# Warm-up matmuls moved behind a data-dependent branch, and GpSimd's row-number copies moved into the first expert's second half

## The chip, the cores and the metric

The kernel runs on one core of a Trainium2 chip. The metric is the device time of one execution in microseconds (us). Three runs of the kernel before gave 944.73, 944.86 and 948.75; the median is 944.86. The engines are named as the profile names them: PE is TensorE (PEld its weight loads), DVE is VectorE, ACT is ScalarE, POOL is GpSimd, SP is SyncE, which here only issues DMAs.

## What is computed

Attention with a sigmoid feeds a layer of eight experts, in which each token goes to exactly one expert by a greedy global ranking, and that feeds a two-matrix block. All inputs and outputs are float32. The parts that matter:

```python
scores = scale * np.matmul(q, k.transpose(0, 1, 3, 2)) - np.log(S)
attn = 1.0 / (1.0 + np.exp(-scores))
x = np.matmul(attn, v)                  # laid out as 1792 tokens x 768
logits = x @ w_gate                     # 8 experts
for idx in np.argsort(-logits.flatten()):
    tok, e = idx // E, idx % E
    if assigned[tok] >= 0 or counts[e] >= cap:   # cap = 224
        continue
    assigned[tok] = e; counts[e] += 1
for e in range(E):
    h = np.maximum(x[assigned == e] @ w1[e], 0.0)
    out[assigned == e] = h @ w2[e]
r = np.maximum(out @ w_in, 0.0)
y = (s * (r * r) + b) @ w_out
```

## The kernel before

The kernel is one long program, placed by hand: every engine works through its instructions in the order in which the source issues them, and semaphores join the engines. Three stages follow each other.

**Attention** (lines 331 to 407, 0 to 165 us). 24 pairs of heads go through scores on PE, a sigmoid on ACT, and values on PE. The first thing that PE does is `keep_clock(WARM[0], ...)`, seven matmuls of zeros whose result nobody reads; the first scores stand behind them.

**Routing** (lines 409 to 620, 165 to 205 us). An auction of ten steps finds the assignment, `places` turns it into row numbers `idx`, and `gather(0)` lets POOL issue two indirect DMAs that fetch the 224 rows of expert 0 into `xr`. Then stands a branch, `go_on`: each engine loads `flag` from memory, and where the auction has not ended (it has, in this profile) the code behind the branch goes on with it. On the way past, each engine adds to its own semaphore what the skipped code would have added (the event semaphores of line 607), so that counts agree on both ways; an instruction behind the branch that waits for DVE's count therefore waits until DVE is past the branch too. Between `places` and the branch PE has `keep_clock(WARM[1], ...)`, 18 matmuls of zeros (line 563).

**Experts and the block** (from line 747, 205 us to the end). Four groups; each has two experts and then the two-matrix block for their 448 rows. Weights are units that come in one fixed order: 8 units of `w1` and 6 of `w2` for an expert, then 32 units of the block. A unit is loaded from memory into `raw` (four buffers), rounded on ACT to `wh` (line 190), and the remainder `wl = raw - wh` is taken on DVE or POOL (line 201), by the table `where`: POOL takes numbers 0, 2, 4, 6 and 12 of an expert's 14 units. A `raw` buffer is free for the next load when its `wl` is done. `advance` issues these steps, always with the unit that is four or five ahead of PE; the units 0 to 3 are split earlier, in the attention, and POOL takes their `wl` there whatever the table says.

In an expert, step f of the first half multiplies unit f with the expert's transposed rows `x` (lines 661, 662; the last two steps lines 680 to 682) and step d of the second half multiplies unit 8 + d with `u`. `x_split(e, n)` transposes a piece of `xr` on PE and splits it on ACT and DVE (lines 653 to 656); expert 0's four pieces stand ahead of its first step, and expert 1's pieces n = 0 to 3 stand behind steps f = 1 to 4 of expert 0, in two buffers `px` of PSUM. Ahead of expert 0 stand `gather(1)` and `row_ids()`. `row_ids` (line 629) is 16 small copies on POOL of `idx` into `idt` and `idl`, which the scatters of finished rows read; the first scatter comes with expert 2.

Of the kernel before, what the change touches and what calls it, by code (L numbers as in the profile page):

```python
# [8 lines left out]
F32 = mybir.dt.float32  # L9
F32R = mybir.dt.float32r  # L10
BF16 = mybir.dt.bfloat16
# [13 lines left out]
CP = 112  # L25
NC = S // CP
NCH = NT // CP
NP = H // 2
KD = DM // 128
KF = F1 // 128  # L30
# [6 lines left out]
STEPS = 10  # L37
MORE = (3, 8)
AHEAD = (2, 3, 4, 5)
WARM = (7, 18, 4, 4)  # L40
ROWS = (3, 3, 2, 2, 2, 2, 2, 2, 2, 2)
SYNC = 0
SIGNS = 2
# [20 lines left out]
def tile_kernel(ctx, tc, qT, kT, v, wg, w1, w2, wi, wo, s2, b2, cst, out):  # L64
# [3 lines left out]
    const = ctx.enter_context(tc.tile_pool(name="const", bufs=1))  # L68
# [17 lines left out]
    ep = early.enter_context(tc.tile_pool(name="ep", bufs=1))  # L86
# [79 lines left out]
    units, where = [], []  # L166
    for g in range(4):
        for e in (2 * g, 2 * g + 1):
            units += [(w1[e, f], KD, True) for f in range(KF)]
            units += [(w2[e, d], KF, True) for d in range(KD)]  # L170
            where += [n in (0, 2, 4, 6, 12) for n in range(KF + KD)]
        units += [(narrow[i], wide[i][1], False) for i in range(len(wide))]
        where += [False] * len(wide)
    raws, splits = {}, {}
# [153 lines left out]
            V.tensor_copy(dv[0][:, 1:], mm[:, 0:1].to_broadcast([128, LEVELS]))  # L328
            V.tensor_scalar(th, kvec, dv[0][:, 1:2], dv[0][:, 0:1], op0=ALU.mult, op1=ALU.add)

    zero = ep.tile([128, 512], BF16, name="zero")
    V.memset(zero, 0.0)

    def keep_clock(n, p):
        for _ in range(n):
            T.matmul(p, zero[:, :CP], zero, start=True, stop=True)

    keep_clock(WARM[0], ps_s.tile([CP, 2, 512], F32, name="psc")[:, 0])
    warm = ep.tile([1, 1], F32, name="warm")
# [32 lines left out]
    for i in range(N):  # L372
        b, p = pairs[i]
# [38 lines left out]
    ps_t = rt.enter_context(tc.tile_pool(name="ps_t", bufs=3, space=PSUM))  # L412
# [147 lines left out]

    auction(STEPS, True)
    places(lambda: rows(len(turns)))
    keep_clock(WARM[1], ps_t.tile([CP, NC, 128], F32, name="px").rearrange("p c n -> p (c n)"))
    def greedy():
        mk = rp.tile([128, CP], F32, name="mk")
        cand = rp.tile([128, CP], F32, name="cand")
# [58 lines left out]
    ps_m = ctx.enter_context(tc.tile_pool(name="ps_m", bufs=6, space=PSUM))  # L625
# [3 lines left out]
    def row_ids():  # L629
        def put(dst, rows, h, col, r0, n, src):  # L630
            for r in range(0, n, 32):
                G.tensor_copy(dst[rows + r:rows + r + 32, col], idx[r0 + r:r0 + r + 32, h, src])

        a, b = slice(0, E, 2), slice(1, E, 2)
        put(idt[:, 0], 0, 0, slice(0, 4), 64, 64, a)
        put(idt[:, 0], 64, 1, slice(0, 4), 0, 64, a)
        put(idt[:, 1], 0, 1, slice(0, 4), 64, 32, a)
        put(idt[:, 1], 32, 0, slice(0, 4), 0, 96, b)
        put(idt[:, 2], 0, 0, slice(0, 4), 96, 32, b)
        put(idt[:, 2], 32, 1, slice(0, 4), 0, 96, b)  # L640
        put(idl, 0, 0, slice(0, 2), 0, 64, slice(0, E, 4))
        put(idl, 64, 0, slice(0, 2), 0, 64, slice(2, E, 4))
# [15 lines left out]
    def half_mm(wh, wl, src, n, func, dst, ahead):  # L658
        p = ps_m.tile([128, 512], F32, name="acc")
        for k in range(n):  # L660
            T.matmul(p[:, :2 * CAP], wh[:, k], src[:, k].rearrange("p a s -> p (a s)"), start=(k == 0), stop=False)  # L661
            T.matmul(p[:, :CAP], wl[:, k], src[:, k, 0], start=False, stop=(k == n - 1))  # L662
        bs = m2p.tile([128, CAP], F32, name="bs")
        A.copy(bs, p[:, CAP:2 * CAP])
        tt = m2p.tile([128, CAP], F32, name="tt")
        V.tensor_add(tt, p[:, :CAP], bs)
        if ahead:
            advance()
        hi, lo = dst
        if func == AF.Relu:  # L670
            A.activation(hi, tt, func)
            V.scalar_tensor_tensor(lo, tt, 0.0, hi.bitcast(F32), op0=ALU.max, op1=ALU.subtract)
        else:
            A.copy(hi, tt)
            V.tensor_sub(lo, tt, hi.bitcast(F32))  # L675
# [19 lines left out]
    def expert(e, y):  # L695
        x = xg.pop(e)
        u = ml.tile([128, KF, 2, CAP], F32R, name="u")
        for f in range(KF):
            wh, wl = w_get()
            if f < KF - 2:  # L700
                half_mm(wh, wl, x, KD, AF.Relu, (u[:, f, 0], u[:, f, 1]), f < KF - 3)
                if f == KF - 3:
                    advance()
            else:
                short_mm(wh, wl, x, KD, (u[:, f, 0], u[:, f, 1]))
                if f == KF - 2:
                    advance()
            if 1 <= f <= 4:
                if e % 2 == 0:
                    x_split(e + 1, f - 1)  # L710
                if out_rows:
                    scatter(*out_rows.pop(0))
        sl = slice((e % 2) * CAP, (e % 2 + 1) * CAP)
        for d in range(KD):
            wh, wl = w_get()
            half_mm(wh, wl, u, KF, AF.Copy, (y[:, d, 0, sl], y[:, d, 1, sl]), d < KD - 1)

    def scatter(ids, row):
        G.memset(spacer, 0.0)
# [25 lines left out]
        late_in()  # L745

    stores, out_rows = [], []
    for n in (0, 2, 1, 3):
        x_split(0, n)
    gather(1)  # L750
    row_ids()
    last["buf"] = ml.tile([128, 3072], I32, name="orow")
    late_in()
    for g in range(4):
# [8 lines left out]
        for f in range(KG):  # L763
            wh, wl = w_get()
            p = ps_m.tile([128, 512], F32, name="acc")
# [22 lines left out]
        for h in range(2):  # L788
            ps = [ps_m.tile([128, 512], F32, name="acc") for _ in tiles]
            n = KG // 2  # L790
# [91 lines left out]
```

## Time and profile before

| what | value |
|---|---|
| median of three runs | 944.86 us |
| the profiled execution, device time | 946.52 us |
| its span, first to last instruction | 944.7 us |
| mean granted clock of PE | 0.983 |
| PE matmuls busy | 917.0 us (97%) |
| PE weight loads busy | 797.0 us (84%) |
| DVE / ACT / POOL busy | 587.6 / 449.3 / 138.1 us |

All times in the rows below are from the profiled execution, which took 946.52 us: 944.7 us of span and 1.8 us around it. Its granted clock is a share of full speed: 1.00 is 2.4 GHz and 0.50 is 1.2 GHz. The page's busy time for PE holds matmuls that wait in its pipeline and so says little about how near PE is to its peak; a stage is read by what its engines wait for.

### The profile page before, as it was taken

To read this page: it belongs to the slowest core of one execution; us is meant where nothing else is said; L and a number is where in the kernel's file an instruction comes from. 1 tells how busy PE (TensorE), PEld (TensorE's weight loads), DVE (VectorE), ACT (ScalarE), POOL (GpSimd) and SP (SyncE) were. 2 spreads that over 40 slices of the span, in tenths; PEclk is the share of its full clock that TensorE was granted. 3 is DMA by queue.
4 is the path that set the end of the run, shared out by engine and by line. 5 is a ranking of instruction groups with operands and counts; after the bars stand their busy time and mean duration, and the time that the engine had idled before them with its cause. 6 is when DMAs were issued, how large, how long until landed. Compare 5 with 4: busy or idle time off the path is not lost.

```text
span 944.7 us, 14521 instructions
## 1 busy us (share of the span) xinstructions
PE 917.0 (97%) x5467; PEld 797.0 (84%) x5467; DVE 587.6 (62%) x1043; ACT 449.3 (48%) x787; POOL 138.1 (15%) x136
## 2 busy tenths in 40 slices
PE   9999999688999999999999999999999999999997
PEld 4454555568999999999999999999999999999997
DVE  3877875645868875578776224786773287777320
ACT  6666767735654432566333225564332366433120
POOL 1000003224410000442000004420000232100001
PEclk9999999779999999999999999999999999999999
DMA  9989993844746666567334235763444476433311
GB/s 307 321 298 341 321 323 111 241 134 167 239 144 214 219 230 217 179 222 230 119 117 141 90 101 165 232 218 122 129 127 137 119 251 211 137 120 108 126 34 68
DMA packets 68459, 173.12 MB, mean 183 GB/s; under 512 B 7968, under 2 KB 24864, under 8 KB 68384
## 3 DMA queue, kind: packets, MB, share of 16 engines
q1 hardware_dynamic: 66112, 161.13, 52.9%
q0 software_dynamic: 2272, 11.01, 3.4%
q8 instruction: 44, 0.72, 0.3%
q14 instruction: 31, 0.25, 0.1%
HBM read 148.52 MB, written 23.59 MB: 182 GB/s over the span
## 4 chain that ended last, share of the span: by engine, by line
PE 56%; DVE 10%; DMA 5%; ACT 3%; issue 2%; POOL 1%; POOLq 0%; SPq 0%; ACTq 0%; DVEq 0%
PE acc L661 9%; PE acc L801 7%; PE acc L802 7%; PE acc L800 7%; PE acc L727 6%; PE acc L728 6%; PE acc L729 6%; PE acc L662 4%; DVE wl L201 4%; DMA raw<-in_w_dram 3%; DMA orow<-in_wo_dram 2%; ACT wh L190 1%; DVE y L675 1%; ACT gt L774 1%; DVE r L770 1%
## 5 line engine op out<-in xcount | busy, mean ns | idle before, releaser
L190 ACT CAST wh<-raw 128x768 fp32r<-128x768 f32 (+1 forms) x240 | 208.8, 877 | 160.6 <-PE acc L802 115.7
L201 DVE TENSOR_TENSOR wl<-raw,wh 128x768 fp32r<-128x768 f32 (+1 forms) x198 | 207.2, 1053 | 91.1 <-ACT wh L190 91.1
L201 POOL TENSOR_TENSOR wl<-raw,wh 128x768 fp32r<-128x768 f32 (+1 forms) x42 | 92.6, 2213 | 414.8 <-ACT wh L190 414.7
L801 PE MATMUL acc<-wl,gt 128*128 128x384 f32 x448 | 150.4, 336 | 1.8 <-DVE wl L201 1.8
L800 PE MATMUL acc<-wh,gt 128*128 128x384 f32 x448 | 150.6, 336 | 0.0
L802 PE MATMUL acc<-wh,gt 128*128 128x384 f32 x448 | 150.4, 336 | 0.0
L727 PE MATMUL acc<-y,wh 128*128 128x448 f32 x384 | 141.4, 368 | 0.0
L729 PE MATMUL acc<-y,wl 128*128 128x448 f32 x384 | 140.6, 366 | 0.0
L728 PE MATMUL acc<-y,wh 128*128 128x448 f32 x384 | 140.6, 366 | 0.0
L661 PE MATMUL acc<-u,wh 128*128 128x448 f32 x384 | 121.9, 376 | 1.8 <-DVE u L685 1.5
L662 PE MATMUL acc<-u,wl 128*128 128x224 f32 x384 | 101.4, 264 | 0.0
L661 PE MATMUL acc<-x,wh 128*128 128x448 f32 x288 | 94.4, 383 | 0.7 <-DVE x L656 0.7
L251 ACT ACTIVATE attn<-psc,nls 112x896 f32<-112x896 f32 x96 | 88.8, 1008 | 9.4 <-PE psc L249 9.4
L769 ACT ACTIVATE r<-acc 128x448 f32<-128x448 f32 x64 | 34.8, 543 | 116.7 <-PE acc L729 116.7
L801 PEld LDWEIGHTS acc<-wl,gt 128*128 128x128 f32 x448 | 84.7, 189 | 2.1 <-DVE wl L201 2.1
L800 PEld LDWEIGHTS acc<-wh,gt 128*128 128x128 f32 x448 | 84.7, 189 | 0.0
L802 PEld LDWEIGHTS acc<-wh,gt 128*128 128x128 f32 x448 | 84.5, 189 | 0.0
L662 PE MATMUL acc<-x,wl 128*128 128x224 f32 x288 | 76.8, 267 | 3.0 <-POOL wl L201 3.0
L661 PEld LDWEIGHTS acc<-u,wh 128*128 128x128 f32 x384 | 72.1, 188 | 8.9 <-DVE u L685 3.6
L260 PE MATMUL pv<-attn,vt 112*64 112x448 f32 x384 | 77.5, 545 | 0.0
L729 PEld LDWEIGHTS acc<-y,wl 128*128 128x128 f32 x384 | 72.1, 188 | 6.3
L728 PEld LDWEIGHTS acc<-y,wh 128*128 128x128 f32 x384 | 72.2, 188 | 6.1
(212 smaller groups left out, 1306.7 us busy)
## 6 DMA issues: line engine op xcount, KB each, us to landing
raw<-nw SPq DMA_DIRECT2D x128, 384.0 KB, 3.0
raw<-in_w_dram SPq DMA_DIRECT2D x64, 384.0 KB, 3.9
raw<-in_w_dram SPq DMA_DIRECT2D x48, 512.0 KB, 4.5
craw<-in_wi_dram SPq DMA_DIRECT2D x16, 768.0 KB, 5.8
nw<-co SPq DMA_DIRECT2D x24, 384.0 KB, 7.7
craw<-in_wo_dram SPq DMA_DIRECT2D x8, 768.0 KB, 6.3
orow<-in_wo_dram SPq DMA_DIRECT2D x8, 768.0 KB
rqk<-in_kT_dram SPq DMA_DIRECT2D x24, 224.0 KB, 6.9
```

The source lines that it names most:

```text
L190: A.copy(h[:, :k], raws[i][:, :k])
L201: eng.tensor_sub(lo[:, :k], r[:, :k], h[:, :k].bitcast(F32))
L251: A.activation(attn[n][:, :, c, :], p[:, :, :S], AF.Sigmoid, bias=nls[:CP], scale=1.0 / math.sqrt(D))
L260: T.matmul(pv[j * 64:(j + 1) * 64, :S], v[:, c, j * D:(j + 1) * D], a[:, j, c, :], start=(c == 0), stop=(c == NC - 1))
L661: T.matmul(p[:, :2 * CAP], wh[:, k], src[:, k].rearrange("p a s -> p (a s)"), start=(k == 0), stop=False)
L662: T.matmul(p[:, :CAP], wl[:, k], src[:, k, 0], start=False, stop=(k == n - 1))
L727: T.matmul(p, wh, src[:, k, 0], start=first, stop=False)
L728: T.matmul(p, wh, src[:, k, 1], start=False, stop=False)
L729: T.matmul(p, wl, src[:, k, 0], start=False, stop=last)
L800: T.matmul(ps[t][:, :DH], hi, wh[:, cols], start=(f == 0), stop=False)
L801: T.matmul(ps[t][:, :DH], hi, wl[:, cols], start=False, stop=False)
L802: T.matmul(ps[t][:, :DH], lo, wh[:, cols], start=False, stop=(f == KG - 1))
```

## The change

Four edits, none of which changes what is computed.

1. `WARM[0]` goes from 7 to 5.
2. The zero matmuls of `WARM[1]` move from ahead of the branch to behind it, directly ahead of expert 0's transposes, and go from 18 to 14. Their operand `zero` moves to a pool that lives that long, and their result goes to a buffer of the experts' PSUM pool.
3. `row_ids()` moves from ahead of expert 0 to behind step d = 1 of expert 0's second half.
4. In the table `where`, POOL gives expert 0's units 0, 2 and 4 to DVE and keeps 6 and 12. Since units 0 to 3 are split in the attention with POOL named outright, unit 4 alone changes its engine.

```diff
-WARM = (7, 18, 4, 4)
+WARM = (5, 14, 4, 4)
...
-            where += [n in (0, 2, 4, 6, 12) for n in range(KF + KD)]
+            where += [n in ((0, 2, 4, 6, 12) if e else (6, 12)) for n in range(KF + KD)]
...
-    zero = ep.tile([128, 512], BF16, name="zero")
+    zero = const.tile([128, 512], BF16, name="zero")
...
     auction(STEPS, True)
     places(lambda: rows(len(turns)))
-    keep_clock(WARM[1], ps_t.tile([CP, NC, 128], F32, name="px").rearrange("p c n -> p (c n)"))
...
             half_mm(wh, wl, u, KF, AF.Copy, (y[:, d, 0, sl], y[:, d, 1, sl]), d < KD - 1)
+            if not e and d == 1:
+                row_ids()
...
+    keep_clock(WARM[1], ps_m.tile([128, 512], F32, name="acc")[:CP])
     for n in (0, 2, 1, 3):
         x_split(0, n)
     gather(1)
-    row_ids()
```

On PE, where the routing ends. Before: the last matmul of `places`, the first zero matmul, the load of the flag and the branch; the skipped code; and the first transpose of expert 0 behind it (the semaphores in brackets are named by engine or DMA queue).

```order
L544 MATMUL pi_2242<-R_1803,oh_1804 96x16
L336 LDWEIGHTS zero_170
L336 MATMUL px_2279<-zero_170 112x512
...
L606 TENSOR_LOAD flag_1798 [waits DMAHW4_49,DMAHW3_49,DMAHW5_49,DMAHW2_49,DMAHW6_49,DMAHW1_49,DMAHW7_49,DMAHW0_49,DVE_49]
L607 COMPARE_AND_BRANCH
...
L653 MATMUL acc_2742<-ident_75,xr_2298 128x128 [waits DMASW0_49,DVE_49,DMASW2_49,PE_49,Activation_49]
```

After, at the same place:

```order
L544 MATMUL pi_2240<-R_1801,oh_1802 96x16
L605 TENSOR_LOAD flag_1796 [waits DMAHW4_49,DMAHW3_49,DMAHW5_49,DMAHW2_49,DMAHW6_49,DMAHW1_49,DMAHW7_49,DMAHW0_49,DVE_49]
L606 COMPARE_AND_BRANCH
...
L336 LDWEIGHTS zero_170 [waits DVE_49,PE_49]
L336 MATMUL acc_2720<-zero_170 112x512 [waits Activation_49]
...
L652 MATMUL acc_2736<-ident_75,xr_2277 128x128 [waits DMASW2_49,DMASW0_49]
```

The zero matmuls now stand between the branch and the transposes, and the waits for DVE's and ACT's counts, which the transposes had, stand at the first of them.

On POOL, from `gather(1)` (two indirect DMAs) to the units that it splits next. Before:

```order
L558 DMA xr_2768<-xs_74,idx_77 96x768 [waits DMASW1_49,DMASW3_49,DVE_49,PE_49]
L632 COPY idt_78<-idx_77 32x4 [waits DMASW5_49,DMASW4_49,Pool_49]
...
L632 COPY idl_79<-idx_77 32x2 x4
L201 TENSOR_TENSOR wl_2834<-raw_1935,wh_2809 128x768 [waits Activation_49,Pool_49]
L201 TENSOR_TENSOR wl_2868<-raw_2013,wh_2838 128x768 [waits PE_49,Activation_49]
L201 TENSOR_TENSOR wl_3071<-raw_2928,wh_3042 128x1024 [waits DVE_49,DMAHW1_49,PE_49,Activation_49]
L201 TENSOR_TENSOR wl_3102<-raw_2988,wh_3075 128x768 [waits DVE_49,DMAHW3_49,PE_49,Activation_49]
```

After:

```order
L558 DMA xr_2762<-xs_74,idx_77 96x768 [waits DMASW1_49,DMASW3_49,DVE_49,PE_49]
L201 TENSOR_TENSOR wl_2846<-raw_2011,wh_2816 128x768 [waits PE_49,Activation_49]
L201 TENSOR_TENSOR wl_3049<-raw_2906,wh_3020 128x1024 [waits DVE_49,DMAHW1_49,PE_49,Activation_49]
L631 COPY idt_78<-idx_77 32x4 [waits DMASW5_49,DMASW4_49,Pool_49]
...
L631 COPY idl_79<-idx_77 32x2 x4
L201 TENSOR_TENSOR wl_3096<-raw_2966,wh_3053 128x768 [waits DVE_49,PE_49,DMAHW3_49,Activation_49,Pool_49]
```

The four subtractions before are units 4, 6, 12 and 14. Unit 4 has left POOL, and the 16 copies stand between unit 12 and unit 14.

On DVE, step f = 1 of expert 0, from its sum `tt` on. Before:

```order
L666 TENSOR_TENSOR tt_2830<-acc_2815,bs_2828 128x224 [waits Activation_49]
L201 TENSOR_TENSOR wl_2836<-raw_1974,wh_2811 128x768
L672 SCALAR_TENSOR_TENSOR u_2789<-tt_2830,u_2789 128x224 [waits Activation_49]
L656 TENSOR_TENSOR x_2842<-px_2843,x_2842 128x3x128 [waits Activation_49]
L666 TENSOR_TENSOR tt_2864<-acc_2849,bs_2862 128x224 [waits Activation_49]
```

After:

```order
L665 TENSOR_TENSOR tt_2808<-acc_2793,bs_2806 128x224 [waits Activation_49]
L201 TENSOR_TENSOR wl_2812<-raw_1933,wh_2787 128x768
L201 TENSOR_TENSOR wl_2814<-raw_1972,wh_2789 128x768
L671 SCALAR_TENSOR_TENSOR u_2767<-tt_2808,u_2767 128x224 [waits Activation_49]
L655 TENSOR_TENSOR x_2820<-px_2821,x_2820 128x3x128 [waits Activation_49]
L665 TENSOR_TENSOR tt_2842<-acc_2827,bs_2840 128x224 [waits Activation_49]
```

Unit 4 stands ahead of unit 5 there, and both ahead of the piece n = 0 of expert 1's rows.

## Rows read from the trace of the kernel before

**Rows 1.** PE's waits, 196 to 275 us: who, for whom, total us, times, longest.

```profile
PE acc L662 <- POOL wl L201: 3.0, 1, 3.0
```

**Rows 2.** Timeline, branch and expert 0: start, length us, engine, line, operation [idle before <-releaser].

```profile
197.94 6.39 PE L336 MATMUL px<-zero 128*112 128x512 bf16 x18
...
200.10 0.22 PEld L336 LDWEIGHTS <-zero 128*112 128x112 bf16 x1 [0.21 <-issue]
...
200.53 0.22 PEld L336 LDWEIGHTS <-zero 128*112 128x112 bf16 x1 [0.21 <-issue]
...
202.66 1.21 PEld L336 LDWEIGHTS <-zero 128*112 128x112 bf16 x6 [0.21 <-issue]
...
204.97 1.35 PE L653 MATMUL acc<-ident,xr 128*128 128x128 f32 x12 [0.63 <-PEq L607]
...
215.57 0.41 PE L653 MATMUL px<-ident,xr 96*128 96x96 f32 x3
```

**Rows 3.** The branch (line 607): engine, durations ns min/median/max, first to last start.

```profile
L607 DVEq EVENT_SEMAPHORE  x2: 21/21/21, 204.1 to 204.2; - x2
L607 PEldq EVENT_SEMAPHORE  x2: 51/51/51, 204.4 to 204.5; - x2
...
L607 PEldq COMPARE_BRANCH  x1: 3342/3342/3342, 199.0 to 199.0; - x1
L607 DVEq COMPARE_BRANCH  x1: 72/72/72, 199.7 to 199.7; - x1
```

**Rows 4.** Windows: stretch, length, busy PE, PEld, DVE, ACT, POOL, then PEclk, DMA, GB/s.

```profile
202.00:203.00 1.00, 1.00 (x5) 0.50 (x4) 0.00 (x0) 0.00 (x0) 0.00 (x0) 0.67 0.85 248
...
204.00:205.00 1.00, 0.37 (x3) 0.07 (x2) 0.00 (x0) 0.00 (x0) 0.00 (x0) 1.00 0.03 8
...
219.00:220.00 1.00, 0.83 (x4) 0.81 (x5) 0.00 (x0) 0.00 (x0) 1.00 (x2) 0.86 0.00 0
220.00:221.00 1.00, 1.00 (x5) 0.91 (x5) 0.00 (x0) 0.00 (x0) 0.90 (x1) 0.50 0.86 205
...
223.00:224.00 1.00, 1.00 (x8) 0.95 (x7) 0.00 (x0) 1.00 (x3) 0.00 (x0) 0.94 0.90 250
```

**Rows 5.** Timeline of POOL alone, 203 to 260 us, columns as in rows 2.

```profile
212.00 3.68 POOL L632 COPY idt<-idx 32x4 int32<-32x4 int32 x12 [3.48 <-DMA xr<-xs,idx]
215.72 0.83 POOL L632 COPY idl<-idx 32x2 int32<-32x2 int32 x4
216.64 4.26 POOL L201 TENSOR_TENSOR wl<-raw,wh 128x768 fp32r<-128x768 f32 x2
233.04 4.76 POOL L201 TENSOR_TENSOR wl<-raw,wh 128x1024 fp32r<-128x1024 f32 x2 [12.14 <-ACT wh L190]
...
247.25 4.16 POOL L201 TENSOR_TENSOR wl<-raw,wh 128x768 fp32r<-128x768 f32 x2 [1.66 <-ACT wh L190]
```

**Rows 6.** Timeline of PE alone, 216 to 246 us, columns as in rows 2.

```profile
219.17 0.37 PE L662 MATMUL acc<-x,wl 128*128 128x224 f32 x1 [2.96 <-POOL wl L201]
...
244.16 0.26 PE L662 MATMUL acc<-x,wl 128*128 128x224 f32 x1
```

**Rows 7.** Timeline of DVE alone, 203 to 260 us, columns as in rows 2.

```profile
211.99 0.95 DVE L201 TENSOR_TENSOR wl<-raw,wh 128x768 fp32r<-128x768 f32 x1
...
213.15 0.55 DVE L656 TENSOR_TENSOR x<-px,x 128x384 fp32r<-128x384 f32 x1
...
249.91 2.31 DVE L201 TENSOR_TENSOR wl<-raw,wh 128x768 fp32r<-128x768 f32 x1
```

**Rows 8.** Timeline of the first 16 us, columns as in rows 2.

```profile
1.19 3.23 PE L336 MATMUL psc<-zero 128*112 128x512 bf16 x7 [1.19 <-DVE zero L332]
...
4.35 5.07 PE L249 MATMUL psc<-rqk 64*112 64x448 f32 x24
...
5.55 5.49 ACT L251 ACTIVATE attn<-psc,nls 112x896 f32<-112x896 f32 x6 [3.32 <-PE psc L249]
```

## The prediction

> **What bounds the kernel now.** I read PE's waits first, then the timeline around the branch and in expert 0, since the whole change lies at the start, at the branch and in expert 0. From 196 to 275 us PE waits 3.0 us for one thing, POOL's `wl` of a weight unit [rows 1]. POOL's own timeline says why it is late: the 16 row-number copies run from 212.00 to 216.55, and only then does POOL begin, at 216.64, the unit that PE stands at [rows 5]. PE goes on at 219.17, after 2.96 us idle [rows 6]. The wait has a tail: PE's granted clock, 1.00 before, is 0.50 in each of the three microseconds from 220 to 223, 0.86 in the one ahead and 0.94 in the one behind [rows 4]. That is 0.28 + 3 + 0.12 = 3.4 us at the 1.2 GHz level, in which 1.7 us are lost. So about 4.7 us hang on that late unit.
>
> At the branch, PE runs its 18 zero matmuls from 197.94 to 204.33, and the transposes of expert 0 follow at 204.97 [rows 2]. The question there is what the zeros cost today. The row of the branch on PE lasts 3342 ns, from 199.0 to 202.3; on DVE it is a short row at 199.7, but DVE's next event comes only at 204.1 [rows 3]. ACT and DVE release nothing behind the branch before that, because DVE's count is short until then. The gather of expert 0's rows is over at about the same time: the DMA share is 0.85 at 202 to 203 and 0.03 at 204 to 205 [rows 4]. So until 204.1 nothing could start anyway, and the 18 zeros are hidden almost whole: without them the transposes could begin perhaps 0.7 us earlier. They also do their work there: the weight loads of the zeros come every 0.43 us at 200.10 and 200.53, the 1.2 GHz pace, and six of them take 1.21 us from 202.66 on, the 2.4 GHz pace [rows 2].
>
> **Zeros behind the branch.** The first zero now waits for DVE's count behind the branch, so it cannot start before 204.1; I take 204.2. DVE's program ahead of the branch is unchanged, and it skips the same code, so I see no reason for it to be past it sooner. From 198 to 204.2 PE idles where it ran the zeros, and the 14 zeros then start at the 1.2 GHz pace of 0.43 us each. How soon the clock rises I take from the three rises in the trace: 4.7 us after the zeros began here (197.94 to 202.66, rows 2), 3.9 us after PE went on in expert 0 (219.17 to about 223.06, rows 4 and 6), and something under the 4.35 us by which the first scores start [rows 8]. With 3.9 us: 9.1 zeros at 0.43 and 4.9 at 0.213 (half of it) are 3.9 + 1.0 = 4.9 us; the transposes begin at 209.1 rather than 204.97, **+4.2 us**. Bounds: 14 zeros at the 1.2 GHz pace are 6.0 us, +5.2; if PE's own branch (over at 202.3) released them, they would begin at 202.4 and cost +2.4; if something still covered them, 0. Nothing hides this: gather(1), the splits and all of expert 0 follow the transposes.
>
> The Trainium skill has a rule that speaks against this edit: "Runtime: NRT & Kernel Launch", section "Instruction fetch mechanics", says that a taken branch whose target is not among the instruction pages at hand has to fetch the page by DMA before the engine goes on. By that rule the gap of 4.4 us on DVE is a fetch that the same program repeats, and PE should keep covering it; the trace agrees as far as PE's row of 3342 ns and DVE's gap go [rows 3]. If only PE's stall counted, the term would be the +2.4 above; by DVE's it is +4.2.
>
> **Row copies and unit 4.** POOL's 16 copies leave the place ahead of expert 0, and unit 4 goes to DVE, in step f = 1. DVE takes a unit of this size in 0.95 us, at 211.99 [rows 7], where now unit 4 stands and unit 5 behind it. So unit 4 is ready at 212.9, long before PE needs it at 216.2, and the 2.96 us and the 1.7 us at the low clock go.
>
> What is late next is DVE. POOL, free of the copies, now takes unit 6 as soon as ACT has rounded it, about 212.4, and works on it for half of 4.26 us, 2.1 us [rows 5], to 214.5. That is beside DVE's unit 5. In expert 1 the same pair is in the trace: DVE's subtraction of this size takes 2.31 us at 249.91 instead of 0.95 [rows 7], while POOL is busy from 247.25 to 251.41 [rows 5]. So unit 5 ends at about 214.5 + 0.9 = 215.4 rather than 212.9, 2.5 us later, and the split of expert 1's piece n = 0, which ended at 213.70 [rows 7], ends at 216.2. Piece n = 2 reuses its PSUM buffer, and PE's transposes of n = 2 stood at 215.57 at the latest [rows 2]. PE waits there some **0.8 us** (bounds 0, if the two do not hinder each other, and 2.3, if the subtraction is held as long as the whole row of 2.31). The sum of this part is -2.96 - 1.7 + 0.8 = **-3.9 us**, bounds -4.7 and -0.7 (2.3 us of wait, which would again bring the clock down).
>
> The Trainium skill ("SBUF — State Buffer", section "SBUF: two separate sides") says that a DVE operation with two SBUF inputs and a GpSimd one that reads SBUF exclude each other, the later one waiting for the whole of the other. The 2.31 us row agrees; without the rule this term would be -4.7.
>
> **Row copies at their new place.** They stand between POOL's units 12 and 14. Unit 12 and unit 14 take 4.76 us together from 233.04 [rows 5]; the first of them ends near 235.8, the copies (4.55 us) end near 240.4, and unit 14 (2.1 to 2.3 us) near 242.6. Expert 1's first `wl` matmul is at 244.16 [rows 6]. So 1.5 us are left, and the cover is expert 0's second half; if it were gone, each microsecond later on POOL would be one of PE. POOL's next unit and gather(2) move back by up to 4.6 us too; gather(2)'s rows are wanted only in the block, 30 us later. The freeing of a `raw` buffer, and so one weight load on SP's queue and those behind it, come later with unit 14, but they had that much slack. I take 0, bounds 0 and +1. The first scatter is in expert 2, far away.
>
> **Five zeros at the start.** The seven run from 1.19 to 4.42 and the first scores start at 4.35 [rows 8]; two fewer free PE 0.85 us earlier, but the scores then wait for their input and may run at the low clock longer. ACT follows from 5.55 without a gap [rows 8] and sets the pace. I take 0; bounds -0.3 (scores at once after their input) and +1.1 (part of the first values at 1.2 GHz).
>
> **The sum.** +4.2 - 3.9 + 0 + 0 = **+0.3 us**. The profiled execution took 946.52, so it would take 946.8. The median of the runs is 944.86, 1.66 below, which is the size of one stretch at the low clock; I apply the difference to the median: **945.2 us**. The expert stage behind is paced by PE and moves as one piece.
>
> **The rivals.**
> - *The zeros stay covered.* For it: PE's branch may come sooner, as no zeros stand ahead of it, and DVE's gap of 4.4 us is an inference from one event. Against it: the wait for DVE's count stands at the first zero. Then only the -3.9 is left: 941.3 us, with bounds of 940.2 (no hindrance on DVE) and 943.4 (PE's own branch counts).
> - *The wait moves from POOL to DVE (slower).* Units 4 and 5 both wait beside POOL's unit 6, and the split of piece n = 0 stands behind both; PE then waits 2.3 us for the PSUM buffer of n = 2 instead of 2.96 for unit 4, and the clock falls as it did. It decides from the point at which DVE's split ends 2 us after PE has come to n = 2. Price against the forecast: 1.5 + 1.7 = 3.2, 948.4 us; with all 14 zeros at the 1.2 GHz pace, 949.4.
> - *The change does not do what it says.* Of "two units of the first expert" only unit 4 moves, which is in the sum already; were the copies not the cause of the late unit, the 3.9 would not come: 949.1 us. The row at 216.64 directly behind the copies speaks against it.
>
> **How the numbers follow.** Forecast (945.2, own range 943.4 to 947.2): 0.70. Zeros covered: 0.15. Wait moves to DVE: 0.10. Gain absent: 0.05. The range reaches down to the covered case and up to the two that end later, with the spread that the runs before show (to 948.75): 941.0 to 949.2. About 0.5% (4.7 us) is what a measurement of this kernel can tell from no change: below 940.1 lies only the lower edge of the covered case, 0.04; above 949.6 only the upper edges of the other two rivals, 0.06; the rest, 0.90, is within.
>
> **What would show it.** In the profile after: PE idle from about 198 to 204.2, then 14 zeros in 4.4 to 6 us, transposes near 209; no wait for a `wl` of POOL in expert 0 and no half-clock stretch there; POOL's copies in the second half of expert 0; a short wait of PE ahead of the transposes of n = 2. I am wrong if the zeros begin before DVE's event behind the branch, if PE waits over 1.5 us in expert 0 or at expert 1's start, or if the attention ends at another time by more than 1 us.

## The result and the profile after

The changed kernel took 951.1 us (median; 946.78 to 955.42) beside 945.04 us for the kernel before on the same chip (942.59 to 948.75). The ratio is 1.0062, with a 95% interval of 1.0045 to 1.0080: slower by about 6 us, where the prediction had +0.3 and a range that ended at 949.2.

| what | before | after |
|---|---|---|
| the profiled execution, device time | 946.52 us | 947.88 us |
| its span | 944.7 us | 946.1 us |
| mean granted clock of PE | 0.983 | 0.980 |
| PE matmuls busy | 917.0 us | 913.3 us |
| DVE / ACT / POOL busy | 587.6 / 449.3 / 138.1 us | 586.5 / 449.7 / 136.8 us |

This profiled execution is one of the shorter of its kernel. A second one (`a_again` below) took 951.52 us, which is near the median.

The waits of PE from 196 to 285 us in the profile after, one line for each pair: who, for whom, total us, times, longest. In [rows 1] one line stood for this stretch up to 275 us, 3.0 us for POOL.

```profile
PE acc L336 <- DVEq L606: 6.3, 1, 6.3
...
PE acc L661 <- DVE wl L201: 1.2, 2, 0.8
PE acc L660 <- DVE u L684: 1.1, 2, 0.9
PE px L652 <- DVE x L655: 0.8, 1, 0.8
```

POOL is gone from it. The first line is the idle stretch at the branch, the last the short wait in expert 0 that the prediction had put at 0.8 us. The two lines between are in expert 1 and are new.

The branch in the profile after: PE's timeline (start, length us, engine, line, operation), then the rows of the branch's line (engine, durations in ns, starts). These answer to [rows 2, 3].

```profile
196.24 2.64 PE L544 MATMUL pi<-R,oh 112*128 112x16 bf16 x32
205.17 4.61 PE L336 MATMUL acc<-zero 128*112 128x512 bf16 x14 [6.28 <-DVEq L606]
209.62 1.32 PE L652 MATMUL acc<-ident,xr 128*128 128x128 f32 x12
211.68 0.47 PE L660 MATMUL acc<-x,wh 128*128 128x448 f32 x1 [0.74 <-DVE x L655]
```

```profile
L606 DVEq EVENT_SEMAPHORE  x2: 21/21/21, 205.0 to 205.1; - x2
...
L606 PEldq COMPARE_BRANCH  x1: 358/358/358, 199.6 to 199.6; - x1
...
L606 DVEq COMPARE_BRANCH  x1: 72/72/72, 200.5 to 200.5; - x1
```

PE's own branch now takes 358 ns, not 3342 [rows 3], and is over at 200.0. It does not help: the first zero stands until DVE's event at 205.0, and the transposes come behind the fourteenth. The 3342 ns are no time that PE's branch needs: in [rows 2, 3] PE's event comes at 204.4, directly behind the last zero, and here, with none ahead, at 200.0.

In expert 0 the half-clock stretch of [rows 4] is gone. The windows of the profile after (stretch, length, busy PE, PEld, DVE, ACT, POOL, then PEclk, DMA, GB/s):

```profile
219.00:220.00 1.00, 1.00 (x8) 0.81 (x6) 1.00 (x2) 0.08 (x1) 0.25 (x1) 1.00 0.78 291
220.00:221.00 1.00, 0.22 (x3) 0.11 (x2) 1.00 (x4) 0.00 (x0) 0.00 (x0) 1.00 0.62 193
```

**Where the time went**, by the starts of the first matmul of each stage on PE. The first column of numbers is from the first of the last routing matmuls (196.24 above) to expert 0's first matmul (211.68); the next two are the lengths of expert 0 and of expert 1, up to the block.

| kernel (profiles) | branch to expert 0 | expert 0 | expert 1 |
|---|---|---|---|
| before | 11.61 | 36.89 | 30.87 |
| before with 5 or 2 zeros at the start (`e4`, `f4`) | 12.00, 11.31 | 35.92, 36.59 | 30.65, 30.67 |
| changed, first and second | 15.44, 15.84 | 32.63, 32.74 | 33.70, 33.97 |
| changed, three more (`p1` to `p3`) | 16.56, 16.90, 14.87 | 32.63 each | 34.11, 33.42, 33.18 |

The means are 11.64, 36.47 and 30.73 for the three kernels with the old order, and 15.92, 32.65 and 33.68 for the five executions of the changed one. So the branch costs +4.3, expert 0 gains 3.8, and expert 1 loses 2.95, where the prediction had nothing. That is +3.4 us of the 5 to 6 in the medians.

Expert 1's loss starts on POOL. Its timeline in the profile after, columns as above, which answers to [rows 5]:

```profile
217.01 2.24 POOL L201 TENSOR_TENSOR wl<-raw,wh 128x768 fp32r<-128x768 f32 x1 [3.86 <-ACT wh L190]
233.40 2.79 POOL L201 TENSOR_TENSOR wl<-raw,wh 128x1024 fp32r<-128x1024 f32 x1 [14.15 <-ACT wh L190]
236.26 3.99 POOL L631 COPY idt<-idx 32x4 int32<-32x4 int32 x12
240.29 1.69 POOL L631 COPY idl<-idx 32x2 int32<-32x2 int32 x4
242.06 3.67 POOL L201 TENSOR_TENSOR wl<-raw,wh 128x768 fp32r<-128x768 f32 x2
```

The 16 copies take 5.7 us here (4.5 in [rows 5]), and unit 14, the first of the pair at 242.06, is done only near 243.9. SP's waits in the profile after, 232 to 250 us; the windows of that stretch; and the row in which ACT goes on:

```profile
SPq L182 <- POOL wl L201: 9.3, 3, 7.3
```

```profile
236.00:240.00 4.00, 4.00 (x28) 3.82 (x27) 2.94 (x7) 2.29 (x6) 3.52 (x12) 1.00 0.46 151
240.00:244.00 4.00, 4.00 (x28) 3.81 (x27) 1.88 (x4) 1.25 (x3) 3.72 (x8) 1.00 0.00 0
244.00:248.00 4.00, 4.00 (x28) 3.81 (x27) 0.00 (x0) 0.78 (x2) 3.55 (x3) 1.00 0.72 248
```

```profile
247.22 0.83 ACT L190 CAST wh<-raw 128x768 fp32r<-128x768 f32 x1 [4.82 <-DMA raw<-in_w_dram]
247.96 0.37 ACT L673 CAST y<-tt 128x224 fp32r<-128x224 f32 x1
```

In the kernel before, the same wait of SP and the same stretch were:

```profile
SPq L182 <- POOL wl L201: 5.6, 4, 1.8
```

```profile
240.00:244.00 4.00, 4.00 (x28) 3.82 (x27) 3.76 (x5) 2.45 (x6) 2.89 (x2) 1.00 0.72 210
```

In the changed kernel SP stands 7.3 us for the `raw` buffer that unit 14 holds, where its longest such wait was 1.8, and from 240 to 244 us no byte of weights moves (DMA share 0.00 in place of 0.72). ACT then waits 4.82 us for the load, with the rounding of `y` queued behind, so DVE has nothing from 244 to 248 (0.00). PE, with a full clock all the while, feels it some microseconds later (its timeline):

```profile
251.12 0.37 PE L661 MATMUL acc<-x,wl 128*128 128x224 f32 x1 [0.79 <-DVE wl L201]
...
255.60 0.37 PE L661 MATMUL acc<-x,wl 128*128 128x224 f32 x1 [0.46 <-DVE wl L201]
...
265.07 0.47 PE L660 MATMUL acc<-u,wh 128*128 128x448 f32 x1 [0.86 <-DVE u L684]
```

### The profile page after: what moved, and what is told of

The parts are those of the page before. It is cut to its first block, busy times and chain, and to the rows that moved or that the text cites. A ratio compares the mean times of both kernels' runs of the same rounds, so it can differ in the third digit from the quotient of the medians.

```text
span 946.1 us, 14506 instructions
## 1 busy us (share of the span) xinstructions
PE 913.3 (97%) x5461; PEld 794.6 (84%) x5461; DVE 586.5 (62%) x1044; ACT 449.7 (48%) x787; POOL 136.8 (14%) x135
## 4 chain that ended last, share of the span: by engine, by line
PE 51%; DVE 12%; DMA 6%; ACT 4%; issue 3%; POOL 1%; POOLq 0%; SPq 0%; ACTq 0%; DVEq 0%
PE acc L802 7%; PE acc L803 7%; PE acc L801 7%; PE acc L728 6%; PE acc L730 6%; PE acc L729 6%; PE acc L660 6%; DVE wl L201 5%; DMA raw<-in_w_dram 4%; PE acc L661 3%; DMA orow<-in_wo_dram 2%; ACT wh L190 2%; DVE y L674 1%; DVE u L671 1%; DVE tt L665 1%
## 5 line engine op out<-in xcount | busy, mean ns | idle before, releaser
L201 DVE TENSOR_TENSOR wl<-raw,wh 128x768 fp32r<-128x768 f32 (+1 forms) x199 | 209.7, 1060 | 89.4 <-ACT wh L190 89.3
L201 POOL TENSOR_TENSOR wl<-raw,wh 128x768 fp32r<-128x768 f32 (+1 forms) x41 | 89.3, 2187 | 417.7 <-ACT wh L190 417.6
```

Source lines behind the costliest of these rows:

```text
L201: eng.tensor_sub(lo[:, :k], r[:, :k], h[:, :k].bitcast(F32))
```

## The experiments

The medians of the kernel before, beside which the runs are compared, were 946.92 (`e1` to `e4`), 946.63 (`e5` to `e7`, `a_again`), 945.56 (`f1` to `f3`) and 946.05 (`f4`, `f5`); ratios are given with their 95% interval. Times of stages are as in the table above, each from one profiled execution.

### Which of the four edits loses

**e1_seven**: the changed kernel with seven zeros at the start.

```diff
-WARM = (5, 14, 4, 4)
+WARM = (7, 14, 4, 4)
```

> The changed kernel with seven zero matmuls at the start again; all else as changed. In the profiles the attention of the changed kernel runs 0.7 us later than before, while the medians are 6 us apart. Theory A (with five zeros PE's clock rises later in many executions and the attention, which PE paces, loses more than the profiled 0.7 us): the median falls from 951.1 to 947 to 948 and the runs lie closer together. Theory B (the start costs only what the profile shows; the rest lies behind the branch): 950.4, with the same spread.

Measured: 949.72, ratio 1.0024 (0.9999 to 1.0048); branch 15.28, expert 0 32.64, expert 1 35.34. The two losses of the table, the longer branch and the longer expert 1, are there with seven zeros too. Neither expected median came: the ratio lies between the two, 2.7 to 3.6 us under the changed kernel's 1.0053 (`a_again`) and 1.0062, with intervals that overlap. So it is not ruled out that the five zeros hold a part of the changed kernel's loss, though no stage of the profiles shows one. The length of expert 1 is not the copies alone: the granted clock is 0.70, 0.50, 0.50 and 0.59 in the four microseconds from 266, which is 3.4 us at the 1.2 GHz level, or 1.7 us lost. PE had waited 0.74 and 0.94 us for `u` ahead of it.

**e2_zeros_ahead**: the changed kernel with 18 zeros ahead of the branch again and none behind.

```diff
-WARM = (5, 14, 4, 4)
+WARM = (5, 18, 4, 4)
...
     places(lambda: rows(len(turns)))
+    keep_clock(WARM[1], ps_t.tile([CP, NC, 128], F32, name="px").rearrange("p c n -> p (c n)"))
...
-    keep_clock(WARM[1], ps_m.tile([128, 512], F32, name="acc")[:CP])
```

> The changed kernel with 18 zero matmuls ahead of the branch again and none behind it; five at the start, copies and unit 4 as changed. Theory A: the transposes of expert 0 begin near 205.5 instead of 209.6 and the time falls by the 4 us of that shift alone, to 947; the spread of the runs stays. Theory B: more than that falls away, 5 to 7 us (944 to 946), and the spread with it.

Measured: 945.74, ratio 0.9983 (0.9956 to 1.0009). The loss is gone. By the medians this edit gives back 6.6 to 7.5 us (from 1.0053 and 1.0062), more than the 3.8 us that the branch stage holds; the interval of 5 us leaves open how much more. The runs still spread over 7.7 us. PE's timeline there, with the zeros ahead of the branch:

```profile
198.69 7.00 PE L336 MATMUL px<-zero 128*112 128x512 bf16 x18
206.25 1.40 PE L653 MATMUL acc<-ident,xr 128*128 128x128 f32 x12 [0.56 <-PEq L607]
```

Branch 12.16, expert 0 32.63, expert 1 33.74: the gain of expert 0 and the loss of expert 1 stay as in the changed kernel, so they belong to the copies and unit 4.

**e7_zeros_behind**: the opposite, the kernel before with 14 zeros behind the branch and nothing else.

```diff
-WARM = (7, 18, 4, 4)
+WARM = (7, 14, 4, 4)
...
-    zero = ep.tile([128, 512], BF16, name="zero")
+    zero = const.tile([128, 512], BF16, name="zero")
...
-    keep_clock(WARM[1], ps_t.tile([CP, NC, 128], F32, name="px").rearrange("p c n -> p (c n)"))
...
+    keep_clock(WARM[1], ps_m.tile([128, 512], F32, name="acc")[:CP])
     for n in (0, 2, 1, 3):
```

> The kernel before with 14 zeros behind the branch in place of 18 ahead of it, and nothing else: seven zeros at the start, row copies ahead of expert 0 and unit 4 on POOL stay. The theory that the zeros behind are the main cost: the transposes of expert 0 come about 13.3 us after the first of the last routing matmuls (9.5 in the kernel before, 10.1 with the zeros ahead in the changed kernel) and the median is 3.3 to 6 us above the kernel before, some 950 to 952. The prediction's own theory: +4.2 from the branch, of which up to 1.7 comes back because the clock stays up in expert 0's first units, so +2.5. The rival theory, that the loss of the changed kernel is in the row copies and the zeros are covered: within 1 us of the kernel before.

Measured: 951.51, ratio 1.0047 (1.0029 to 1.0065): by the median this edit alone loses about as much as all four. Its branch takes 15.51 us to expert 0; PE's timeline:

```profile
205.70 4.64 PE L336 MATMUL acc<-zero 128*112 128x512 bf16 x14 [6.33 <-DVEq L606]
210.18 1.32 PE L652 MATMUL acc<-ident,xr 128*128 128x128 f32 x12
```

Expert 0 keeps its wait for POOL, here 3.2 us, and takes 37.02. Expert 1 took 34.47 in this execution, the longest of its eleven, with ACT 2.54 us behind one weight load and again 3.4 us at the 1.2 GHz level (0.53, 0.50, 0.50 and 0.76 from 270 us); nothing here shows whether that goes with the edit.

**f1_four_behind**: the changed kernel with 4 zeros behind the branch.

```diff
-WARM = (5, 14, 4, 4)
+WARM = (5, 4, 4, 4)
```

> The changed kernel with 4 zeros behind the branch in place of 14. By the theory that each zero behind the branch delays expert 0 by its own length (14 took 4.6 us, 0.33 each): transposes 10.1 us behind the first of the last routing matmuls (13.4 with 14, 9.5 to 10.1 with none there) and 3.3 us less by the median, 947 to 948. By the rival, that the delay is the wait for the vector engine's count behind the branch, whatever the number of zeros: transposes at 12 or later and less than 1.5 us gained. A third: the 14 zeros keep the clock up, and with 4 expert 0 begins at half clock and gives the 3.3 us back: expert 0 takes 35 us or more instead of 32.7.

Measured: 948.64, ratio 1.0034 (1.0014 to 1.0053). PE's timeline:

```profile
204.34 1.92 PE L336 MATMUL acc<-zero 128*112 128x512 bf16 x4 [5.78 <-DVEq L606]
206.06 1.95 PE L652 MATMUL acc<-ident,xr 128*128 128x128 f32 x12
```

Branch 12.57 us, 3.3 less than the mean of the changed kernel, for ten zeros fewer; expert 0 took 32.64, so the ten bought nothing there. The ratio falls from 1.0053 and 1.0062 to 1.0034, which is 1.8 to 2.6 us, with intervals that overlap. In the branch it is the number of zeros that costs; the wait for DVE (5.78 here) hides none of them. Expert 1 took 34.86 in this execution, more than in any of the changed kernel, with the clock at 0.50 for three microseconds from 262 and 0.81 in the next.

**e4_five_alone**: the kernel before with five zeros at the start; **f4_two_start**: with two.

```diff
-WARM = (7, 18, 4, 4)
+WARM = (5, 18, 4, 4)
```

```diff
-WARM = (7, 18, 4, 4)
+WARM = (2, 18, 4, 4)
```

> The kernel before with five instead of seven zero matmuls at the start, nothing else. Theory A: 3 us or more above the kernel before (948 or more), with a wider spread. Theory B: 0.7 us above, 945.7.

> The kernel before with 2 zeros at the start in place of 7, and nothing else. Open is whether fewer zeros at the start put off the moment at which the matrix engine's pace doubles; the profiles so far had the first values at 9.4 to 10.5 us with seven zeros and at 9.7 to 11.9 with five. If they do: with two the first values come at 11.5 us or later, everything behind moves with them, and the median is 1.5 us or more above the kernel before. If not (the moment varies from one execution to the next whatever the zeros): first values at 9.4 to 10.5 us and the median within 1 us of the kernel before.

Measured: 945.79, ratio 0.9979 (0.9954 to 1.0003), and 946.6, ratio 1.0004 (0.9985 to 1.0023). Neither loses. The 24 first score matmuls show how soon PE's pace doubles: 5.07 us in [rows 8] with seven zeros, and in PE's timeline of the changed kernel, of its second execution, and of the kernel with two zeros, one line each:

```profile
4.03 6.05 PE L249 MATMUL psc<-rqk 64*112 64x448 f32 x24 [0.46 <-DMA rqk<-in_qT_dram]
```

```profile
4.10 7.38 PE L249 MATMUL psc<-rqk 64*112 64x448 f32 x24 [0.53 <-DMA rqk<-in_qT_dram]
```

```profile
4.09 6.73 PE L249 MATMUL psc<-rqk 64*112 64x448 f32 x24 [1.80 <-DMA rqk<-in_qT_dram]
```

Two executions of one and the same kernel differ by 1.3 us here, nearly as much as kernels with seven, five and two zeros do (5.07 to 6.73). Over all profiles the first values come at 9.3 to 11.9 us with five zeros (mean 10.3 of twelve) and at 9.4 to 10.5 with seven (10.1 of six); with two they came at 10.8, between the two times expected. That makes a part of the spread between runs, and in the profiles no part of the loss that can be told from it.

### What the row copies cost, and where

**e3_copies_ahead**: the changed kernel with the copies back ahead of expert 0.

```diff
-            if not e and d == 1:
-                row_ids()
...
     gather(1)
+    row_ids()
```

> The changed kernel with the row-number copies ahead of expert 0 again (unit 4 stays on DVE, zeros and start as changed). If the copies behind POOL's unit 12 hold unit 14, with it the next raw buffer and SP's queue, and so cost the 2.8 us by which expert 1 is longer in the changed profile: expert 1 takes 30.9 us again rather than 33.7, PE's wait for the buffer of piece n = 2 (0.8 us) goes too, and the time falls by 2.8 to 3.6 us, to 947.5 to 948.3. If expert 1 is longer for another reason (the shift against the weight loads), it stays at 33.7 us and the time does not fall.

Measured: 952.24, ratio 1.0052 (1.0028 to 1.0076). The fall of 2.8 to 3.6 us did not come. Expert 1 fell to 31.48 as expected, but expert 0 rose to 38.06 (the profiled execution, of 958.04, is the longest of the twelve). POOL's unit 6 now stands behind the copies and frees its `raw` buffer late: SP stands 6.5 us for POOL and ACT 4.90 us for the load. The `u` of the second half come late, PE waits for them 0.94, 0.86 and 0.50 us, and the clock falls. The windows of this kernel:

```profile
234.00:236.00 2.00, 1.00 (x3) 0.72 (x4) 2.00 (x4) 2.00 (x4) 0.00 (x0) 0.89 0.15 61
236.00:238.00 2.00, 1.50 (x5) 1.03 (x5) 0.95 (x2) 0.04 (x1) 0.00 (x0) 0.50 0.76 246
238.00:240.00 2.00, 2.00 (x8) 1.83 (x8) 1.52 (x2) 1.97 (x3) 0.60 (x1) 0.50 0.70 207
```

So, by the medians, moving the copies away was worth about as much as it cost: 5.7 to 5.9 us of copies on POOL hold a weight load at either place.

**f2_copies_mid**: the changed kernel with the copies in expert 1, behind POOL's units 14 to 20, where POOL then idles.

```diff
+            if e == 1 and f == 6:
+                row_ids()
...
-            if not e and d == 1:
-                row_ids()
```

> The changed kernel with the row copies in expert 1, behind POOL's units 14 to 20 and ahead of unit 26, where POOL was idle for 12 us; zeros stay behind the branch. By the theory that what the copies cost is that POOL's unit 14, and with it SP's next raw loads, stand behind them: expert 1 falls from 33.8 to 30.7 to 31.6 us and the median by 2 to 3 us, to 948 to 949. By the rival, that the copies cost wherever they stand ahead of the block, or that the late start behind the zeros is what makes expert 1 late: it stays at 33 us or more, and the time at 951.

Measured: 948.28, ratio 1.0028 (1.0009 to 1.0047). Expert 1 took 31.07 us in place of 33.7, with the branch as late as ever (16.96). SP's longest wait for POOL in the same stretch, the window from 240 to 244 us, and the copies on POOL:

```profile
SPq L182 <- POOL wl L201: 4.3, 3, 1.8
```

```profile
240.00:244.00 4.00, 4.00 (x27) 3.82 (x27) 3.55 (x7) 2.12 (x6) 1.23 (x1) 1.00 0.68 203
```

```profile
253.26 5.29 POOL L631 COPY idt<-idx 32x4 int32<-32x4 int32 x12
258.60 0.84 POOL L631 COPY idl<-idx 32x2 int32<-32x2 int32 x4
266.00 2.73 POOL L201 TENSOR_TENSOR wl<-raw,wh 128x1024 fp32r<-128x1024 f32 x1 [6.56 <-ACT wh L190]
```

The load runs through (0.68 for 0.00) and 6.56 us of idle time follow the copies. This is the mechanism of expert 1's loss: the copies themselves cost nothing, the `raw` buffer behind them does.

**e5_copies_late**: the kernel before with the copies behind expert 1 and unit 4 on DVE; zeros as in the kernel before.

```diff
-            where += [n in (0, 2, 4, 6, 12) for n in range(KF + KD)]
+            where += [n in ((0, 2, 4, 6, 12) if e else (6, 12)) for n in range(KF + KD)]
...
     gather(1)
-    row_ids()
...
         expert(2 * g + 1, y)
+        if not g:
+            row_ids()
```

> The kernel before with the row copies put behind expert 1 of group 0, where POOL has no unit to multiply, and unit 4 of expert 0 on DVE; zeros at the start and ahead of the branch as in the kernel before. The theory that the copies hold POOL's unit 14 and with it SP's raw load: with the copies there no longer, expert 1 takes about 30.9 us (33.7 in the changed kernel, 30.9 before), the first half of expert 0 still 17.6 us (21.65 before), so 3 to 4 us below the kernel before: 942 to 943. The rival theory, that unit 4 moved to DVE is what makes expert 1 late, whatever the copies do: expert 1 stays at 33 us or more, and the time is 945 to 946. A third: the copies hold the block of group 0 instead, which then starts or ends its first part 2 us or more later, 944 to 946.

Measured: 941.33, ratio 0.9947 (0.9929 to 0.9964): faster than both kernels. Branch 12.22, expert 0 32.63, expert 1 31.58. On POOL the copies stand in front of an idle stretch:

```profile
264.97 5.26 POOL L632 COPY idt<-idx 32x4 int32<-32x4 int32 x12
270.26 0.84 POOL L632 COPY idl<-idx 32x2 int32<-32x2 int32 x4
```

**e6_no_unit6**: as that, with unit 6 of expert 0 on DVE as well.

```diff
-            where += [n in ((0, 2, 4, 6, 12) if e else (6, 12)) for n in range(KF + KD)]
+            where += [n in ((0, 2, 4, 6, 12) if e else (12,)) for n in range(KF + KD)]
```

> As the run with the copies behind expert 1, with unit 6 of expert 0 on DVE too, so that POOL takes only unit 12 there. The theory that DVE's unit 5 is slowed by sharing its time with POOL's unit 6, which makes the matrix engine wait 0.8 us for a px buffer: that wait goes and the first half of expert 0 is some 0.8 us shorter than 17.6. The rival: DVE has then one unit more to do (2.4 us) in the same time and becomes the one waited for, and expert 0's first half is 1 to 2 us longer. Beside the run without it: 0.8 us below by the one, 1 to 2 above by the other.

Measured: 941.17, ratio 0.9937 (0.9916 to 0.9959). Expert 0 took 31.85 and has no wait for the `px` buffer, 0.78 us less. DVE's timeline shows units 4 and 5 with POOL idle beside them:

```profile
213.15 1.82 DVE L201 TENSOR_TENSOR wl<-raw,wh 128x768 fp32r<-128x768 f32 x2
```

They take 1.82 us here and 3.47 in the changed kernel, beside POOL's unit 6 (shown further down): that unit did slow them. In the medians the step is too small to be told from none.

### Whether the zeros at the branch are of use

**f3_no_zeros**: as the last, with no zeros around the branch at all; **f5_none_five**: that with five zeros at the start.

```diff
-WARM = (7, 18, 4, 4)
+WARM = (7, 0, 4, 4)
```

```diff
-WARM = (7, 0, 4, 4)
+WARM = (5, 0, 4, 4)
```

> The run with the copies behind expert 1 and units 4 and 6 on DVE, without any zeros around the branch (18 ahead of it before). By the theory that the zeros ahead of the branch bring the clock up for expert 0: without them the matrix engine begins expert 0 at half clock and it takes 2 us or more longer than 31.9, 943 to 944. By the rival, that the clock rises as soon without them or that they delay the branch on the matrix engine: the same time or 1 us less, 940 to 941.

> The run without zeros around the branch (copies behind expert 1, units 4 and 6 on DVE) with five zeros at the start in place of seven, beside which nothing differs. That run was 5.2 us below the kernel before. If five at the start cost something in the median, though not in every execution: 2 us or more are lost of this. If not: 4.5 to 6 us below the kernel before, as with seven.

Measured: 940.73, ratio 0.9945 (0.9925 to 0.9965), and 943.7, ratio 0.9963 (0.9944 to 0.9982). In the first, PE's timeline:

```profile
205.16 2.47 PE L653 MATMUL acc<-ident,xr 128*128 128x128 f32 x12 [6.46 <-DVEq L607]
207.60 0.74 PE L661 MATMUL acc<-x,wh 128*128 128x448 f32 x1
```

The branch falls to 11.55 us, and expert 0 (32.69, with matmuls of 0.60 us up to 209.5) is 0.84 us longer than with 18 zeros ahead of the branch. One gives back about half of the other, 0.45 for 0.84 us, and the medians do not tell the two kernels apart. The difference between seven and five at the start (a ratio of 1.0018, 1.7 us) is inside the two intervals and fits neither expectation; it stays open.

### The same kernels once more

**a_again**, **p1_after**, **p2_after**, **p3_after** (the changed kernel) and **p4_zeros_ahead** (`e2_zeros_ahead`), unchanged, for more executions with a trace.

> The changed kernel once more, beside the others on one chip, for a second profiled execution. By the theory that the zeros behind the branch cost 3.3 to 4 us, that the later copies take back 2.8 of the 4 us that expert 0 gains, and that the rest varies with when the clock rises at the start: 947 to 951 us by the median, transposes of expert 0 13.3 us behind the last routing matmuls' start, expert 1 33.7 us. By the rival theory, that the loss is of one execution alone: the transposes' distance or the length of expert 1 differs by over 1 us from the first profile.

> The changed kernel, one more profiled execution. Open is what the medians hold beyond the steps: zeros behind the branch +3.3 to +4.2, expert 0 -4.2, expert 1 +2.8 to +3.1, together about +2 to +3, against +5 to +6 in the medians. One theory: in part of the executions the clock falls to half for some 3.4 us in expert 1, as it did in three kernels with zeros behind (expert 1 of 34.5 to 35.3 us instead of 33.7). The other: the pace doubles late at the start (first values at 11 us or later instead of 10.0).

> As the run before it: by the one theory expert 1 takes 34.5 us or more, by the other the first values come at 11 us or later; where neither is seen, the execution takes 947 to 949.

> As the two runs before it: which stage holds what is over 949 us.

> The changed kernel with its 18 zeros ahead of the branch again, one more profiled execution. First values at 9.7 to 11.9 us as with any five zeros at the start, transposes 10.1 us behind the last routing matmuls' start, expert 1 33.7 us with no half-clock stretch; 943 to 947.

Measured: `a_again` 951.95, ratio 1.0053 (1.0034 to 1.0072); the single executions 949.78, 948.5 and 949.48, and 948.74 for the zeros ahead, beside one of 948.85 of the kernel before, too few for a ratio. The stages stand in the table. The zeros vary most, by PE's clock while they run: 0.50 from 206 to 210 us in `p2_after`, but 0.76 from 206 to 208 and 1.00 from 208 to 210 in `p3_after`. PE's timelines of the two:

```profile
204.72 6.19 PE L336 MATMUL acc<-zero 128*112 128x512 bf16 x14 [6.16 <-DVEq L606]
```

```profile
204.26 4.52 PE L336 MATMUL acc<-zero 128*112 128x512 bf16 x14 [5.80 <-DVEq L606]
```

Neither of the two theories for the rest held: in the three `p` runs the first values came at 9.3 to 9.7 us, and expert 1 took 33.2 to 34.1 with no stretch at half clock. `p4_zeros_ahead` missed its range (943 to 947) and both its stages: the transposes came 8.7 us behind the routing matmuls for the expected 10.1, and PE waited 1.43 us for `xr` in the middle of them, so the branch still took 12.07. Expert 0 (34.06) and expert 1 (35.44) were longer than in `e2_zeros_ahead`: in the first the clock fell directly behind that wait (0.84, 0.50 and 0.81 in the steps of 2 us from 208, or 1.7 us lost), in the second PE waited 2.5 us for a `wl` of DVE. So expert 1 can be long with no zeros behind the branch too.

## Why the prediction was wrong

One step failed, the row copies taken at nothing; the other terms held in the traces. That step alone does not make the miss: with it at its measured size the forecast would have been about 948.2, and 2 to 3 us of the median are in no stage.

- **Zeros behind the branch, +4.2.** Right in mechanism and size. PE idled until DVE's count (predicted 204.2; 205.17 in the profile after, where the routing's last matmuls already start 0.8 us later), the 14 zeros took 4.5 to 6.2 us (predicted 4.9, bound 6.0, which one execution passed), and the branch lost +4.3 in the mean. The edit alone costs 0.47%, and with ten zeros fewer the branch is 3.3 us shorter. The rival that they stay covered is out: PE's branch does come sooner (358 ns), and DVE's count decides. DVE's gap, 4.4 us in [rows 3], is 4.5 here (200.5 to 205.0) with nothing on PE ahead of it, and 3.9 to 4.7 over all the profiles. The rule of the Trainium skill ("Runtime: NRT & Kernel Launch", section "Instruction fetch mechanics"), as the prediction used it, had the same program repeat this gap, and the trace agrees; that the gap is a fetch, no run here shows. The reading of PE's row as a branch over at 202.3 was wrong, and with it the bound of +2.4: without zeros ahead PE is past at 200.0. The price of this rival should also read 941.0, which is 944.86 - 3.9; the 941.3 takes the 3.9 from the forecast.
- **Unit 4 and POOL's wait, -3.9.** Right: expert 0 went from 36.89 to 32.63, -4.26 against that profile and -3.8 against the mean of three. POOL's wait and the half-clock stretch are gone, and the wait for the `px` buffer is 0.78 us (predicted 0.8). DVE's timeline and PE's show its origin, the two units that share their time with POOL's unit 6 at 217.01:

```profile
216.60 3.47 DVE L201 TENSOR_TENSOR wl<-raw,wh 128x768 fp32r<-128x768 f32 x2
...
220.29 0.55 DVE L655 TENSOR_TENSOR x<-px,x 128x384 fp32r<-128x384 f32 x1
```

```profile
220.89 0.47 PE L652 MATMUL px<-ident,xr 96*128 96x96 f32 x3 [0.78 <-DVE x L655]
```

- **Row copies at their new place, 0 (bound +1).** This step failed: it cost +2.8 in the first profile and +2.95 in the mean. The prediction reckoned when unit 14's `wl` is wanted by PE, found 1.5 us left, and let the `raw` buffer and SP's queue go with "they had that much slack", for which it names no row. The traces show none: SP stood 7.3 us for that buffer, ACT 4.82 us for the load, and three waits of PE followed, the last some 20 us on. That the copies took 5.7 instead of 4.55 us was the smaller part. `f2_copies_mid` shows the step by taking it away: the same copies, 17 us later, and expert 1 is 2.6 us shorter than the changed kernel's mean.
- **Five zeros at the start, 0.** Not refuted: five alone and even two alone cost nothing that can be measured in the kernel before. In the changed kernel seven zeros took 2.7 to 3.6 us off the median (`e1_seven`), with intervals that overlap, so a cost there is not excluded.
- **The sum.** +4.3 - 3.8 + 2.95 is +3.4, in place of +0.3. The medians say +5 to +6, with intervals that begin at +3.2 (1.0034) and +4.3 (1.0045), so 2 to 3 us stay without a stage, and their cause is open. The five profiled executions of the changed kernel average 949.4, some 2 us under its medians of 951.1 and 951.95, so what is missing lies in part in executions that left no trace. Two candidates are on record and neither is shown: the stretch of 3.4 us at the 1.2 GHz level in expert 1, which `e1_seven`, `e7_zeros_behind` and `f1_four_behind` have and those five have not, and the zeros at the start. The kernel before, over all its runs beside the experiments, has medians of 945.0 to 946.9, up to 2 us above the 944.86 that the forecast was laid on; in the ratio this has no part.
- **The range.** It ended 4.0 us above the forecast, and the median lies 5.9 above it. The bound of +1 on the copies had no row under it; their own length, 4.55 us, was the bound to hold while no slack was proved. It covers the +2.95 that was measured, but not the 2 to 3 us without a stage.
- **The rivals.** None came true. The one that ended slower put the new wait on DVE in expert 0, by 2.3 us; the wait there was 0.78, and the larger new one came one expert later, by way of SP.

## What to carry to other kernels

When work is moved on an engine that also frees buffers, follow each buffer it holds to the queue that fills it, and to who waits for that load; the time until its own result is wanted is not the slack. Work that only keeps an engine busy belongs where the engine idles anyway: ahead of a wait that another engine sets 18 zeros cost 0.45 us in the branch, behind it each piece cost its own length. An improvement can be hidden by its own placement: with the copies where POOL idles and the zeros left alone, the same idea is 0.5% faster than the kernel before (941.33, ratio 0.9947).

## What the runs showed of the hardware

- DVE is past the branch 3.9 to 4.7 us after its own branch row over all the profiles, whether PE runs zeros meanwhile (3.9 to 4.7) or nothing (4.0 to 4.6). PE, with no zeros ahead, has a branch row of 352 to 358 ns and is past at once. Behind 18 zeros its row lasted from 236 ns (`f4_two_start`) to 3912 ns (`e4_five_alone`), and its event came as the last zero ended each time (204.4 after 204.3 in the kernel before).
- Twelve copies of 32x4 numbers took 2.9 to 4.2 us on POOL ahead of expert 0 (3.68 in [rows 5]), 3.8 to 4.0 between the weight units, and 5.3 in stretches where they were expected to run alone: 0.24 to 0.44 us each. What makes the difference stays open.
- The same 14 zeros took 4.5 to 6.2 us from one execution to the next, and the first 24 scores 5.3 to 7.4 us in the changed kernel alone, by when the pace doubles. One profiled execution can sit 3 us off the median, as the first one here does.
